# Gates of the first batch joined to the second's, ranks beside counts, independent stores, late records

## The chip, the cores and the metric

One core of a Trainium2 chip runs the whole program. The metric is the device time of one execution in microseconds (us). TensorE (PE) multiplies, VectorE (DVE), ScalarE (ACT) and GpSimd (POOL) do elementwise work, SyncE (SP) issues most of the DMAs. PSUM is the memory that TensorE writes, SBUF the one that all engines read.

## The reference

```python
scores = scale * np.matmul(q, k.transpose(0, 1, 3, 2)) - np.log(S)   # (8, 12, 448, 448), head_dim 64
attn = 1.0 / (1.0 + np.exp(-scores))
x = np.matmul(attn, v)            # then laid out as (3584, 768): 8 batches of 448 tokens
logits = x @ w_gate               # 8 experts
expert_idx = np.argmax(logits, axis=1)
gate_w = probs[np.arange(N), expert_idx]          # softmax of the logits
for e in range(E):                # w1 (8, 768, 1024), w2 (8, 1024, 768)
    mask = expert_idx == e
    out[mask] = gate_w[mask, None] * (np.maximum(x[mask] @ w1[e], 0.0) @ w2[e])
```

## The kernel before

**Attention.** Twelve heads make six pairs a batch. Two pairs advance together in steps of 64 keys, seven steps (ST) to two pairs, 21 (PB) to a batch, 168 in all; a step is called s below. `scores(s)` multiplies 64 by 64 quarters of k with 448 columns of q into two PSUM tiles named sc, `squash` makes the sigmoid on ScalarE, `weighted(s)` multiplies with v into av. `tokens` transposes av on VectorE into xt and writes it to x_tok in DRAM; `copy_tokens` keeps a copy in SBUF for the logits. `turn` transposes k and q on VectorE.

**Gates.** For each batch b: `gate_a` makes the logits (24 records on TensorE, line 291), `gate_b` transposes them (two matmuls, L300) and finds each token's expert (oh, one hot) on VectorE, `gate_c` counts the tokens of each expert with a matmul over ones (L335), finds the commonest expert and says which batch fills the next dense slot, `gate_c2` marks which tokens go elsewhere (lm), `gate_c3` makes the gate factors. `gate_d` numbers the tokens that go elsewhere: two matmuls into pr, one over the upper triangle for the rank within a group, one over ones for the totals (L388, L389), and a chain of additions on VectorE that reads pr (L392 to L403). `gate_d2` scatters four records per batch with GpSimd (L424). The small PSUM tiles of these steps share the four buffers of sc.

**Experts.** Seven dense slots (NS) each hold one batch's 448 tokens and the commonest expert of it. `moe` works in three passes of 128 by 128 matmuls over split weights (high and low part): L240 for the first layer, L263 for the second. ScalarE makes the high part of a weight, GpSimd the low one (L160). L247 and L248 free an expert PSUM tile (two buffers) and make the high and low part of the hidden values. What stays over is done at the end by lists of records.

**Order.** Everything is in an order written out by hand: `attention` yields, and `more(7)` puts seven expert matmuls in between. Before s = 70 (START) there are no expert matmuls; after it, seven steps of attention come in one burst (i == BURST), and expert matmuls fill the rest. PLACES says at which s a gate step stands: EARLY for the first two batches (first batch: b at 26, c and c2 at 28, c3 at 30, d at 32, its records at 34 to 40; second batch: b at 48, c at 50, the tokens' load l and c3 at 52, d at 54, records from 56 to 62), FIRST_LATE and LATE for the next five, LAST for the eighth. Each engine, and SyncE's queue, works in the order of the program. `store` issues an output store on SyncE; it waits for earlier stores unless `apart` has declared the two independent, which it does for stores of the same columns. `tokens` issues four writes of x_tok on SyncE as soon as a batch's half is transposed.

Of the kernel before, what the change touches and what calls it, by code (L numbers as in the profile page):

```python
# [9 lines left out]
F32 = mybir.dt.float32  # L10
F32R = mybir.dt.float32r
BF16 = mybir.dt.bfloat16
# [6 lines left out]
P = 128  # L19
NCH = 4  # L20
# [4 lines left out]
def tile_sigmoid_attention_top1_moe(  # L25
# [182 lines left out]
                self.split += 1  # L208

    stores = []  # L210
    stored = {}
# [12 lines left out]
    def moe(b, wts):  # L224

# [60 lines left out]
    def gate_a(b):  # L286
        psg = small_ps(b, "psg")
        for t in range(KD):
            for h in range(2):
                n = t % 2 * 2 + h  # L290
                nc.tensor.matmul(
                    psg[32 * n : 32 * (n + 1), :GH], wg[:, t], wholes[b, t][:, h * GH : (h + 1) * GH],
                    start=(t < 2), stop=(t >= KD - 2),
                )
        nc.vector.tensor_copy(logits, psg[:, :GH])

    def gate_b(b):
        pl = small_ps(b, "pl")
# [28 lines left out]
    def gate_c(b, oh, z):  # L327
        def tl(nm, shape, dt=F32):
            return small.tile(shape, dt, tag=nm, name=f"{nm}_{b}")

        s1, s2 = tl("s1", [GP, NCH, E]), tl("s2", [GP, NCH, E])
        nc.scalar.activation(s1, z, AF.Sigmoid)
        nc.scalar.activation(s2, z, AF.Sigmoid, scale=-1.0)
        pc = small_ps(b, "pc")
        nc.tensor.matmul(pc[:, : NCH * E], ones[:GP], oh.rearrange("p c e -> p (c e)"), start=True, stop=True)  # L335
        cnt = tl("cnt", [P, E])
        nc.vector.tensor_reduce(cnt, pc[:, : NCH * E].rearrange("p (c e) -> p e c", e=E), axis=AX.X, op=ALU.add)
        cm = tl("cm", [P, 1])
        nc.vector.tensor_reduce(cm, cnt, axis=AX.X, op=ALU.max)
        ce = tl("ce", [P, E])  # L340
        nc.vector.scalar_tensor_tensor(ce, cnt, cm, rev, op0=ALU.is_equal, op1=ALU.mult)
        cr, was, now = top[:, b : b + 1], free[:, b : b + 1], free[:, b + 1 : b + 2]
        nc.vector.tensor_reduce(cr, ce, axis=AX.X, op=ALU.max)
        ri = tl("ri", [P, 2], I32)
        if b > 0:
            rf = tl("rf", [P, 2])
            old = top[:, b - 1 : b]
            nc.vector.tensor_sub(rf[:, 0:1], old, cr)
            nc.vector.scalar_tensor_tensor(rf[:, 0:1], rf[:, 0:1], was, cr, op0=ALU.mult, op1=ALU.add)
            nc.vector.tensor_scalar(ri[:, 0:1], rf[:, 0:1], -1.0, float(E), op0=ALU.mult, op1=ALU.add)  # L350
            nc.vector.tensor_scalar(ri[:, 1:2], was, -1.0, float(b), op0=ALU.mult, op1=ALU.add)
        return s1, s2, ri, ce, cm

    def gate_c2(b, oh, s1, s2, ri, ce, cm):
# [12 lines left out]
        nc.vector.tensor_scalar(ce, ce, keep, 1.0, op0=ALU.mult, op1=ALU.add)  # L367
        lm = tl("lm", [GP, NCH, E], BF16)
        nc.vector.tensor_tensor(lm, oh, ce[:GP].unsqueeze(1).broadcast_to([GP, NCH, E]), op=ALU.mult)
        return lm  # L370

    def gate_c3(b, s1, s2):
        nc.vector.reciprocal(s2, s2)
# [6 lines left out]
    def gate_d(b, lm):  # L380
# [10 lines left out]
        tot = pr[:, nce : 2 * nce].rearrange("p (c e) -> p c e", e=E)  # L391
# [12 lines left out]
        return si  # L404
# [47 lines left out]
    xts = {}  # L452
    wholes = {}
    raws = {}
    taken = [[] for _ in range(4)]
    x_tok_b = x_tok.rearrange("(b j r) (i f) -> b i r j f", b=B, r=32, i=4)

    def load_slot(n, ri):

        regs[n] = nc.sync.value_load(ri[0:1, 0:1], min_val=0, max_val=E - 1)  # L460
        maps[n] = nc.sync.value_load(ri[0:1, 1:2], min_val=0, max_val=B - 1)
        raws[n] = xpool.tile([P, S // 32, KD, 32], F32, tag="raw", bufs=1, name=f"raw_{n}")
        for i in range(4):
            got = nc.sync.dma_start(
                raws[n][32 * i : 32 * (i + 1)].rearrange("r j t s -> r j (t s)"),
                x_tok_b[bass.ds(maps[n], 1), i].rearrange("o r j f -> (o r) j f"),
            )
            taken[i].append(got)

    low_parts = []  # L470

# [16 lines left out]
    def tokens(g, pv):  # L488
# [5 lines left out]
            xts[b] = xtpool.tile([P, NB, KH, 32], F32, tag="xt", bufs=2, name=f"xt_{b}_{n}")  # L494
        nc.vector.transpose(xts[b][:, :, t, :], pv[:, :S].rearrange("p (j s) -> p j s", s=32))  # L495
        if t == KH - 1:
            rows = x_tok[b * S : (b + 1) * S].rearrange("(j r) (i f) -> i r j f", r=32, i=4)
            for i in range(4):
                put = nc.sync.dma_start(
                    rows[i][:, :, n * KH * 32 : (n + 1) * KH * 32],  # L500
                    xts[b][32 * i : 32 * (i + 1)].rearrange("r j t s -> r j (t s)"),
                )
# [170 lines left out]
    def attention():  # L673
# [32 lines left out]

        def stage(what, b):
            g = gate.setdefault(b, {})
            if what == "b":
                g["oh"], g["z"] = gate_b(b)  # L710
            elif what == "c":
                g["c"] = gate_c(b, g["oh"], g["z"])
# [4 lines left out]
            elif what == "l" and b > 0:  # L717
                load_slot(b - 1, g["c"][2])
            elif what == "d":
                si_of[b] = gate_d(b, g["lm"])  # L720
# [6 lines left out]

        LATE = {8: "b", 10: "c", 11: ("l", "c2"), 12: "c3", 15: "d", 16: "g", 26: "e"}
        FOUR = ("s0", "s1", "s2", "s3")
        PUTS = 2 * (dict(zip((13, 15, 17, 19), FOUR)),) + 4 * (dict(zip((27, 28, 29, 30), FOUR)),)  # L730
        PUTS += (dict(zip((25, 26, 27, 28), FOUR)), {9: "s0", 10: "s1"})
        LAST = {3: "b", 5: "c", 6: ("l", "c2"), 7: "c3", 8: "d", 9: "g"}
        EARLY = {5: "b", 7: ("c", "c2"), 9: ("l", "c3"), 11: "d", 13: "g", 32: "e"}
        FIRST_LATE = {8: "b", 10: "c", 11: ("l", "c2"), 12: "c3", 15: "d", 16: "g", 26: "e"}
        PLACES = {}
        for b in range(B):
            places = (EARLY, EARLY, FIRST_LATE, LATE, LATE, LATE, LATE, LAST)[b]
            for r, what in [*places.items(), *PUTS[b].items()]:
                at = (b + 1) * PB + r
                at += at < START and at % 2  # L740
# [19 lines left out]
        for s in range(N_ST + 11):  # L760
# [33 lines left out]
            if s in SPLITS:  # L794
                split_tokens(0, SPLITS.index(s), nc.vector.tensor_copy)
            yield s, MIX[1]
        order.close()

    wts = Weights([(lambda b=b: regs.get(b)) for b in range(B + 1)], NS)
# [382 lines left out]
```

## Time and profile before

| what | value |
|---|---|
| time of three runs | median 776.97 us (776.0 to 777.6) |
| the profiled execution | 776.84 us, span 775.0 us |
| PE busy | 768.4 us (99%), 5586 matmuls |
| DVE, ACT, POOL busy | 373.9, 384.1, 349.6 us (48%, 50%, 45%) |
| PE clock granted | 1.000 |
| DMA | 125.67 MB, 162 GB/s |

The span runs from the first to the last instruction; the profiled execution's time has 1.84 us around it. A matmul's end in the trace is modelled, so the busy share says little about how densely the matmuls follow each other: the starts do. An fp32 matmul is recorded twice.

### The profile page before, as it was taken

The numbers are of one execution on the slowest core, as the hardware profiler recorded it, in microseconds if no ns is written. First come the engines' busy times: TensorE is split into PE (matmuls) and PEld (weight loads), VectorE is DVE, ScalarE is ACT, GpSimd is POOL, SyncE is SP. The second block draws the span as 40 slices with busy tenths as digits, with TensorE's granted clock in tenths as the row PEclk, the third lists the DMA queues.
The fourth block names the chain that finished last, engine by engine and source line by source line (L and its number), as shares of the span: only waits on it lengthen the run. The fifth ranks groups of instructions, "written<-read, shape, count | busy, mean of one in ns | idle before, by whom it ended". The sixth has DMA issues, their size and how long they took to land. (4 is left out here: it accounts for less than half of the span.)

```text
span 775.0 us, 15532 instructions
## 1 busy us (share of the span) xinstructions
PE 768.4 (99%) x5586; PEld 593.3 (77%) x5586; DVE 373.9 (48%) x806; ACT 384.1 (50%) x688; POOL 349.6 (45%) x330
## 2 busy tenths in 40 slices
PE   9999999999999999999999999999999999999997
PEld 6555557687696786867868769677698999999996
DVE  2354584465264652537426384254736493244543
ACT  5877776645536455264443653545523342444451
POOL 8648554242352342531615316054265764664351
PEclk9999999999999999999999999999999999999999
DMA  9777798976758846587585876766167554655770
GB/s 207 169 160 157 171 251 197 210 171 154 169 129 173 201 107 166 139 190 168 116 194 84 193 169 144 183 168 166 38 171 170 157 146 118 202 143 155 220 223 38
DMA packets 311633, 125.67 MB, mean 162 GB/s; under 512 B 210062, under 2 KB 307006, under 8 KB 311552
## 3 DMA queue, kind: packets, MB, share of 16 engines
q1 hardware_dynamic: 305504, 112.42, 61.9%
q0 software_dynamic: 5760, 11.76, 5.4%
q8 instruction: 45, 0.74, 0.4%
q10 hardware_dynamic: 288, 0.46, 0.2%
q14 instruction: 36, 0.29, 0.1%
HBM read 102.49 MB, written 22.49 MB: 161 GB/s over the span
## 5 line engine op out<-in xcount | busy, mean ns | idle before, releaser
L602 ACT ACTIVATE at<-sc,bias_s 128x448 f32<-128x448 f32 x336 | 192.3, 633 | 107.4 <-PE sc L616 106.5
L160 POOL TENSOR_TENSOR w1l<-wst,w1h 128x768 fp32r<-128x768 f32 x72 | 132.7, 1853 | 173.9 <-ACT w1h L159 172.2
L160 POOL TENSOR_TENSOR w2l<-wst,w2h 128x512 fp32r<-128x512 f32 x84 | 107.0, 1298 | 138.7 <-ACT w2h L159 121.0
L616 PE MATMUL sc<-qt,kt 64*64 64x448 f32 x1344 | 167.3, 545 | 0.0
L632 PE MATMUL av<-at,vn 64*64 64x448 f32 x1344 | 165.0, 536 | 0.0
L240 PE MATMUL ps<-xh,w1h 128*128 128x448 f32 x336 | 124.4, 370 | 0.2 <-DVE nw L439 0.2
L240 PE MATMUL ps<-xh,w1l 128*128 128x448 f32 x336 | 123.4, 367 | 0.0
L240 PE MATMUL ps<-xl,w1h 128*128 128x448 f32 x336 | 123.3, 367 | 0.0
L263 PE MATMUL ps<-hh,w2l 128*128 128x448 f32 x336 | 123.3, 367 | 0.0
L263 PE MATMUL ps<-hl,w2h 128*128 128x448 f32 x336 | 123.2, 367 | 0.0
L263 PE MATMUL ps<-hh,w2h 128*128 128x448 f32 x336 | 122.7, 365 | 0.0
L616 PEld LDWEIGHTS sc<-qt,kt 64*64 64x64 f32 x1344 | 78.2, 189 | 56.9 <-issue 44.4
L632 PEld LDWEIGHTS av<-at,vn 64*64 64x64 f32 x1344 | 59.4, 133 | 64.3 <-issue 53.5
L159 ACT CAST w2h<-wst 128x512 fp32r<-128x512 f32 x108 | 64.7, 620 | 75.7 <-PE ps L263 64.5
L247 ACT ACTIVATE hh<-ps 128x448 fp32r<-128x448 f32 x56 | 30.6, 546 | 139.6 <-PE ps L240 137.0
L276 DVE TENSOR_TENSOR ps<-ps,gt 128x448 f32<-128x448 f32 x42 | 40.7, 969 | 85.4 <-PE ps L263 85.3
L495 DVE STREAM_TRANSPOSE xt<-av 128x448 f32<-128x448 f32 x46 | 27.3, 629 | 101.5 <-PE av L632 100.4
L248 DVE SCALAR_TENSOR_TENSOR hl<-ps,hh 128x448 fp32r<-128x448 f32 x56 | 34.4, 614 | 78.3 <-ACT hh L247 76.8
L240 PEld LDWEIGHTS ps<-xh,w1h 128*128 128x128 f32 x336 | 63.1, 188 | 9.9 <-issue 4.4
L263 PEld LDWEIGHTS ps<-hh,w2l 128*128 128x128 f32 x336 | 65.2, 194 | 6.6 <-issue 3.5
L263 PEld LDWEIGHTS ps<-hl,w2h 128*128 128x128 f32 x336 | 65.2, 194 | 6.2 <-issue 3.2
L263 PEld LDWEIGHTS ps<-hh,w2h 128*128 128x128 f32 x336 | 65.2, 194 | 3.4 <-DVE nw L439 0.2
(158 smaller groups left out, 918.9 us busy)
## 6 DMA issues: line engine op xcount, KB each, us to landing
wst<-in_moe_w_dram SPq DMA_DIRECT2D x72, 384.0 KB, 3.3
wst<-in_moe_w_dram SPq DMA_DIRECT2D x54, 512.0 KB, 5.1
x_tok<-xt SPq DMA_DIRECT2D x64, 168.0 KB, 2.8
qn<-in_q_dram SPq DMA_DIRECT2D x184, 56.0 KB, 3.1
raw<-x_tok SPq DMA_DIRECT2D x28, 336.0 KB, 6.2
out_dram<-ob SPq DMA_DIRECT2D x84, 112.0 KB, 2.4
kn<-in_k_dram SPq DMA_DIRECT2D x104, 56.0 KB, 3.3
kn<-in_k_dram POOLq DMA_DIRECT2D x80, 56.0 KB, 4.0
```

The source lines that it names most:

```text
L159: nc.scalar.copy(hi, st)
L160: eng.tensor_tensor(lo, st, hi.bitcast(F32), op=ALU.subtract)
L240: nc.tensor.matmul(ps[:, :S], a[:, ws], b_, start=(t == 0 and n == 0), stop=(t == KD - 1 and n == 2))
L247: nc.scalar.activation(hh[:, :S], ps[:, :S], AF.Relu)
L248: nc.vector.scalar_tensor_tensor(hl[:, :S], ps[:, :S], 0.0, hh[:, :S].bitcast(F32), op0=ALU.max, op1=ALU.subtract)
L263: nc.tensor.matmul(ps[:, :S], a, b_, start=(j == 0 and n == 0), stop=(j == KF - 1 and n == 2))
L276: nc.vector.tensor_tensor(by_gate, by_gate, gate_rows[b], op=ALU.mult)
L495: nc.vector.transpose(xts[b][:, :, t, :], pv[:, :S].rearrange("p (j s) -> p j s", s=32))
L602: nc.scalar.activation(at, ps[:, :S], AF.Sigmoid, bias=bias_s, scale=SCALE)
L616: nc.tensor.matmul(ps[quarter(g, h), :S], ks, ops[g, "q"][OWN[h]], start=True, stop=True)
L632: nc.tensor.matmul(psv[g][OWN[h], :S], ops[g, "v"][rows, c, :], at[rows], start=(c == 0), stop=(c == KC - 1))
```

## The change

Of the first batch only the logits are made at its place (into logits_0). The second batch's places do all other gate steps for both: four transposes, operations over twice the columns, two counting matmuls, no rank matmuls. In batches 3 to 8 the rank matmul runs beside the counting one, over oh instead of lm, and the results are copied to SBUF (sums). The records of the first batch move from s = 34, 36, 38, 40 to 70, 72, 74, 76, those of the second from 56 to 62 to 80, 82, 84, 86. All output stores are declared independent of each other, all token writes of all token loads; the token writes are issued behind the next seven expert matmuls. An empty instruction on SyncE stands ahead of each store and each group of token writes. The working tiles of the joined steps lie in two buffers that the hidden values use later (h0).

```diff
     def store():
...
+            nc.sync.nop()
             put = nc.sync.dma_start(
...
-            apart(put, stored.setdefault((d, i), []))
+            apart(put, stored)
...
-        nc.vector.tensor_copy(logits, psg[:, :GH])
+        nc.vector.tensor_copy(logits_0 if b == 0 else logits, psg[:, :GH])
...
+    def early_b():
+        pl = small_ps(1, "pl")
+        for b, lo in enumerate((logits_0, logits)):
+            for c in range(2):
+                at = (2 * b + c) * P
+                nc.tensor.transpose(pl[:GP, at : at + P], lo[:, c * GP : (c + 1) * GP], ident)
...
+    def early_c(oh, z):
...
+        for n, of in enumerate((ones, upper)):
+            nc.tensor.matmul(
+                pc[:, n * n2 : (n + 1) * n2], of[:GP], oh.rearrange("p c e -> p (c e)"), start=True, stop=True
+            )
+        sums = early[1][:, GH : GH + 2 * n2]
+        nc.vector.tensor_copy(sums, pc[:, : 2 * n2])
...
-        nc.tensor.matmul(pc[:, : NCH * E], ones[:GP], oh.rearrange("p c e -> p (c e)"), start=True, stop=True)
+        nce = NCH * E
+        for n, of in enumerate((ones, upper)):
+            nc.tensor.matmul(
+                pc[:, n * nce : (n + 1) * nce], of[:GP], oh.rearrange("p c e -> p (c e)"), start=True, stop=True
+            )
+        sums = tl("sums", [P, 2, NCH, E])
+        nc.vector.tensor_copy(sums.rearrange("p n c e -> p (n c e)"), pc[:, : 2 * nce])
...
+        nc.vector.tensor_mul(cnt, cnt, ce)
...
-        pr = small_ps(b, "pr")
-        lmf = lm.rearrange("p c e -> p (c e)")
-        nce = NCH * E
-        nc.tensor.matmul(pr[:, :nce], upper[:GP], lmf, start=True, stop=True)
-        nc.tensor.matmul(pr[:, nce : 2 * nce], ones[:GP], lmf, start=True, stop=True)
...
-            nc.vector.tensor_add(pre[:, c], pre[:, c - 1], tot[:, c - 1])
-        nc.vector.tensor_add(base, pre[:, NCH - 1], tot[:, NCH - 1])
+            nc.vector.tensor_add(pre[:, c], pre[:, c - 1], sums[:, 0, c - 1])
+        nc.vector.tensor_add(base, base, cnt)
...
-        nc.vector.tensor_add(rk, pre[:GP], pr[:GP, :nce].rearrange("p (c e) -> p c e", e=E))
+        nc.vector.tensor_add(rk, pre[:GP], sums[:GP, 1])
...
+            to_keep.append((b, n, xts[b]))
...
+    def keep_tokens():
+        while to_keep:
+            b, n, xt = to_keep.pop(0)
...
-                for got in taken[i]:
+                for got in taken:
                     tc.declare_no_dep(put.ins, got.ins, reason="the slots read earlier batches' tokens")
...
-        PUTS = 2 * (dict(zip((13, 15, 17, 19), FOUR)),) + 4 * (dict(zip((27, 28, 29, 30), FOUR)),)
+        PUTS = tuple(dict(zip(range(r, r + 8, 2), FOUR)) for r in (START - PB, START + 10 - 2 * PB)) + 4 * (dict(zip((27, 28, 29, 30), FOUR)),)
...
-        EARLY = {5: "b", 7: ("c", "c2"), 9: ("l", "c3"), 11: "d", 13: "g", 32: "e"}
+        EARLY = {5: "B", 7: "C", 9: ("l", "C3"), 11: "D", 13: "g", 32: "e"}
...
-            places = (EARLY, EARLY, FIRST_LATE, LATE, LATE, LATE, LATE, LAST)[b]
+            places = ({}, EARLY, FIRST_LATE, LATE, LATE, LATE, LATE, LAST)[b]
...
             yield s, MIX[0]
+            keep_tokens()
```

## Rows read from the trace of the kernel before

**Rows 1.** Waits of TensorE, whole span: total us, times, longest.

```profile
PE ps_warm L593 <- DVE ones L76: 1.1, 1, 1.1
PE ps L240 <- DVE nw L439: 0.2, 1, 0.2
```

**Rows 2.** Timeline of TensorE, first batch's gates: start us, us, instructions, count.

```profile
45.09 1.34 PE L291 MATMUL psg<-xf,wg 128*32 128x224 f32 x24
46.36 1.79 PE L616 MATMUL sc<-qt,kt 64*64 64x448 f32 x16
...
49.61 0.43 PE L300 MATMUL pl<-ident,logits 128*112 128x128 f32 x2
49.97 1.79 PE L616 MATMUL sc<-qt,kt 64*64 64x448 f32 x16
...
63.21 2.02 PE L616 MATMUL sc<-qt,kt 64*64 64x448 f32 x16
...
76.74 1.27 PE L632 MATMUL av<-at,vn 64*64 64x448 f32 x8
...
81.74 1.34 PE L291 MATMUL psg<-xf,wg 128*32 128x224 f32 x24
```

**Rows 3.** The same, first row of the stretch that ends at 45.09 (rows 2).

```profile
11.55 1.66 PE L616 MATMUL sc<-qt,kt 64*64 64x448 f32 x12
```

**Rows 4.** The same, first row and end of the second batch's stretch.

```profile
83.01 1.79 PE L616 MATMUL sc<-qt,kt 64*64 64x448 f32 x16
...
115.71 1.34 PE L291 MATMUL psg<-xf,wg 128*32 128x224 f32 x24
```

**Rows 5.** The same, third batch's counting and rank matmuls among expert matmuls.

```profile
135.85 0.37 PE L240 MATMUL ps<-xh,w1h 128*128 128x448 f32 x1
136.06 0.19 PE L335 MATMUL pc<-oh,ones 112*128 112x32 bf16 x1
...
136.38 0.37 PE L240 MATMUL ps<-xh,w1l 128*128 128x448 f32 x1
...
161.37 0.37 PE L240 MATMUL ps<-xl,w1h 128*128 128x448 f32 x1
161.58 0.19 PE L388 MATMUL pr<-lm,upper 112*128 112x32 bf16 x1
...
161.93 0.36 PE L240 MATMUL ps<-xh,w1h 128*128 128x448 f32 x1
```

**Rows 6.** The same, first and last rows of stretches of 55 expert matmuls.

```profile
149.90 0.47 PE L240 MATMUL ps<-xh,w1h 128*128 128x448 f32 x1
...
244.41 0.47 PE L240 MATMUL ps<-xh,w1h 128*128 128x448 f32 x1
...
255.66 0.37 PE L240 MATMUL ps<-xl,w1h 128*128 128x448 f32 x1
```

**Rows 7.** Timelines of VectorE (alone, beside a split) and GpSimd (the split).

```profile
87.40 0.19 DVE L317 TENSOR_TENSOR eq<-lg,mx 112x32 f32<-112x32 f32 x1
...
131.52 1.45 DVE L317 TENSOR_TENSOR eq<-lg,mx 112x32 f32<-112x32 f32 x1
...
131.09 1.84 POOL L160 TENSOR_TENSOR w1l<-wst,w1h 128x768 fp32r<-128x768 f32 x1 [5.13 <-ACT w1h L159]
```

**Rows 8.** Timelines: a late operation of a rank chain; an expert tile's release and use.

```profile
352.19 1.20 DVE L399 TENSOR_TENSOR rk<-rk,lm 112x32 f32<-112x32 f32 x1
...
259.34 0.58 DVE L248 SCALAR_TENSOR_TENSOR hl<-ps,hh 128x448 fp32r<-128x448 f32 x1
...
259.97 0.48 PE L263 MATMUL ps<-hh,w2h 128*128 128x448 f32 x1
```

**Rows 9.** Waits of SyncE's queue, the longest: total us, times, longest.

```profile
SPq L218 <- DMA out_dram<-ob: 82.2, 50, 5.9
```

**Rows 10.** Timelines of VectorE and TensorE ahead of the first expert matmuls.

```profile
102.47 1.18 DVE L495 STREAM_TRANSPOSE xt<-av 128x448 f32<-128x448 f32 x2 [2.02 <-PE av L632]
...
117.46 0.62 DVE L570 STREAM_TRANSPOSE qt<-qn 128x448 f32<-128x448 f32 x1
...
120.10 1.70 PE L616 MATMUL sc<-qt,kt 64*64 64x448 f32 x16
```

**Rows 11.** Busy time of VectorE in that stretch: us, DVE busy (operations), clock, DMA.

```profile
102.47:118.08 15.61, 15.20 (x29) 1.00 1.14 258
```

More of the change, by code (lines that the diff above doesn't have):

```diff
@@ L294, in gate_a, with both @@
                 )
-        nc.vector.tensor_copy(logits, psg[:, :GH])
+        nc.vector.tensor_copy(logits_0 if b == 0 else logits, psg[:, :GH])
+    early = [hpool.tile([P, 2 * S], F32, tag=f"h{x}0", name=f"early_{x}") for x in "hl"]
+    logits_0 = early[1][:, :GH]
+    cuts = {}
+    def both(nm, n, words=None):
+        if nm not in cuts:
+            at = cuts.get("at", 0)
+            cuts[nm], cuts["at"] = early[0][:, at : at + (words or n)], at + (words or n)
+            assert cuts["at"] <= 2 * S
+        return cuts[nm]
@@ new lines, in both_e, with per_c, bc @@
+    def both_e(nm, n=1):
+        return both(nm, 2 * NCH * E).rearrange("p (c e) -> p c e", e=E)
+    def per_c(ce):
+        return ce[:GP].rearrange("p (b e) -> p b e", e=E).unsqueeze(2).broadcast_to([GP, 2, NCH, E])
+    def early_b():
[4 more added lines that the diff above has]
+                nc.tensor.transpose(pl[:GP, at : at + P], lo[:, c * GP : (c + 1) * GP], ident)
+        plv = pl[:GP].rearrange("p (c t h e) -> p c t h e", c=4, t=2, h=2)
+        sh = [GP, 2 * NCH, E]
+        def bc(a):
+            return a.unsqueeze(2).broadcast_to(sh)
+        lg, eq, z = (both_e(nm)[:GP] for nm in ("lg", "eq", "z"))
+        mx, mr = (both(nm, 2 * NCH)[:GP] for nm in ("mx", "mr"))
+        oh = both("oh", 2 * NCH * E, NCH * E).bitcast(BF16).rearrange("p (c e) -> p c e", e=E)[:GP]
+        lgv = lg.rearrange("p (c h) e -> p c h e", c=4)
+        nc.vector.tensor_copy(lgv, plv[:, :, 0, :, :E])
+        nc.vector.tensor_add(lgv, lgv, plv[:, :, 1, :, :E])
+        nc.vector.tensor_reduce(mx, lg, axis=AX.X, op=ALU.max)
+        nc.vector.tensor_tensor(eq, lg, bc(mx), op=ALU.is_equal)
+        nc.vector.tensor_tensor(eq, eq, rev[:GP].unsqueeze(1).broadcast_to(sh), op=ALU.mult)
+        nc.vector.tensor_reduce(mr, eq, axis=AX.X, op=ALU.max)
+        nc.vector.tensor_tensor(oh, eq, bc(mr), op=ALU.is_equal)
+        nc.vector.tensor_tensor(z, lg, bc(mx), op=ALU.subtract)
+        return oh, z
@@ new lines, in early_c @@
+    def early_c(oh, z):
+        s1, s2 = (both_e(nm)[:GP] for nm in ("s1", "s2"))
+        nc.scalar.activation(s1, z, AF.Sigmoid)
+        nc.scalar.activation(s2, z, AF.Sigmoid, scale=-1.0)
+        pc = small_ps(1, "pc")
+        n2 = 2 * NCH * E
+        for n, of in enumerate((ones, upper)):
[4 more added lines that the diff above has]
+        nc.vector.tensor_copy(sums, pc[:, : 2 * n2])
+        sums = sums.rearrange("p (n b c e) -> p n b c e", n=2, b=2, e=E)
+        cnt, cm, ce, keep = both("cnt", 2 * E), both("cm", 2), both("ce", 2 * E), both("keep", 2)
+        cnt_b, ce_b = (x.rearrange("p (b e) -> p b e", e=E) for x in (cnt, ce))
+        sh = [P, 2, E]
+        nc.vector.tensor_reduce(cnt_b, sums[:, 0].rearrange("p b c e -> p b e c"), axis=AX.X, op=ALU.add)
+        nc.vector.tensor_reduce(cm, cnt_b, axis=AX.X, op=ALU.max)
+        nc.vector.tensor_tensor(ce_b, cnt_b, cm.unsqueeze(2).broadcast_to(sh), op=ALU.is_equal)
+        nc.vector.tensor_tensor(ce_b, ce_b, rev.unsqueeze(1).broadcast_to(sh), op=ALU.mult)
+        nc.vector.tensor_reduce(top[:, :2], ce_b, axis=AX.X, op=ALU.max)
+        for b in range(2):
+            was, now, kept = free[:, b : b + 1], free[:, b + 1 : b + 2], keep[:, b : b + 1]
+            nc.vector.scalar_tensor_tensor(kept, cm[:, b : b + 1], float(2 * P), was, op0=ALU.is_le, op1=ALU.mult)
+            nc.vector.tensor_sub(now, was, kept)
+        rf = both("rf", 1)
+        ri = small.tile([P, 2], I32, tag="ri", name="ri_1")
+        was = free[:, 1:2]
+        nc.vector.tensor_sub(rf, top[:, 0:1], top[:, 1:2])
+        nc.vector.scalar_tensor_tensor(rf, rf, was, top[:, 1:2], op0=ALU.mult, op1=ALU.add)
+        nc.vector.tensor_scalar(ri[:, 0:1], rf, -1.0, float(E), op0=ALU.mult, op1=ALU.add)
+        nc.vector.tensor_scalar(ri[:, 1:2], was, -1.0, 1.0, op0=ALU.mult, op1=ALU.add)
+        return ri, oh, ce, keep, cnt, sums
@@ new lines, in early_c2 @@
+    def early_c2(oh, ce, keep, cnt):
+        ce_b = ce.rearrange("p (b e) -> p b e", e=E)
+        nc.vector.tensor_tensor(ce_b, ce_b, top[:, :2].unsqueeze(2).broadcast_to([P, 2, E]), op=ALU.is_equal)
+        nc.vector.tensor_scalar(keep, keep, -1.0, None, op0=ALU.add)
+        for b in range(2):
+            nc.vector.tensor_scalar(ce_b[:, b], ce_b[:, b], keep[:, b : b + 1], 1.0, op0=ALU.mult, op1=ALU.add)
+        lm = both("lm", 2 * NCH * E).rearrange("p (b c e) -> p b c e", b=2, e=E)[:GP]
+        nc.vector.tensor_tensor(lm, oh.rearrange("p (b c) e -> p b c e", b=2), per_c(ce), op=ALU.mult)
+        nc.vector.tensor_mul(cnt, cnt, ce)
+        return lm
@@ L297, in gate_b, with early_c3 @@
+    def early_c3():
+        s1, s2 = (both_e(nm)[:GP] for nm in ("s1", "s2"))
+        nc.vector.reciprocal(s2, s2)
+        nc.vector.tensor_mul(s1, s1, s2)
+        sm = both("sm", 2 * NCH)[:GP]
+        nc.vector.tensor_reduce(sm, s1, axis=AX.X, op=ALU.add)
+        nc.vector.tensor_scalar(sm, sm, 1e-9, None, op0=ALU.add)
+        nc.vector.reciprocal(gates[:GP, :2].rearrange("p b c -> p (b c)"), sm)
     def gate_b(b):
@@ L367, in gate_c2 @@
         nc.vector.tensor_scalar(ce, ce, keep, 1.0, op0=ALU.mult, op1=ALU.add)
-        lm = tl("lm", [GP, NCH, E], BF16)
+        lm = tl("lm", [GP, NCH, E])
         nc.vector.tensor_tensor(lm, oh, ce[:GP].unsqueeze(1).broadcast_to([GP, NCH, E]), op=ALU.mult)
-        return lm
+        nc.vector.tensor_mul(cnt, cnt, ce)
+        return lm, sums, cnt
     def gate_c3(b, s1, s2):
@@ L454, in tile_sigmoid_attention_top1_moe @@
     raws = {}
-    taken = [[] for _ in range(4)]
+    taken = []
     x_tok_b = x_tok.rearrange("(b j r) (i f) -> b i r j f", b=B, r=32, i=4)
@@ L708, in stage @@
             g = gate.setdefault(b, {})
-            if what == "b":
+            if what == "B":
+                g["oh"], g["z"] = early_b()
+            elif what == "C":
+                ri, *g["early"] = early_c(g["oh"], g["z"])
+                g["c"] = None, None, ri
+            elif what == "C3":
+                oh, ce, keep, cnt, sums = g["early"]
+                g["lm"] = early_c2(oh, ce, keep, cnt)
+                early_c3()
+            elif what == "D":
+                oh, ce, keep, cnt, sums = g["early"]
+                for n in range(2):
+                    si_of[n] = gate_d(n, g["lm"][:, n], sums[:, :, n], cnt[:, n * E : (n + 1) * E])
+            elif what == "b":
                 g["oh"], g["z"] = gate_b(b)
@@ L796, in attention @@
             yield s, MIX[1]
+        keep_tokens()
         order.close()
```

19 lines of the change are left out of this document (10 added, 9 removed).

## The prediction

> **What bounds the kernel now.** I read the waits of TensorE first. In the whole span it waits 1.3 us for another engine, 1.1 of it once at the start [rows 1]. So VectorE, ScalarE, GpSimd and the DMA queues end no stretch of it. The end moves only with the time TensorE itself needs, or if one of the others becomes late.
>
> The second view is TensorE's timeline, read for its pitch, because a busy share of 99% does not show a matmul that takes longer than it must. In the attention stage an undisturbed stretch, from 63.21 to 76.74, starts 144 score and value matmul records in 13.53 us: 0.094 us each [rows 2]. Against that pitch I measure every stretch between two logit matmuls. From 46.36 to 81.74 (first batch: its three small gate steps lie in it) 352 records start in 35.38 us; at the pitch they need 33.06, so 2.32 us are lost [rows 2]. From 11.55 to 45.09, where no gate matmul lies, 350 records take 33.54 and need 32.88: 0.66 lost [rows 3]. From 83.01 to 115.71 (second batch) 320 records take 32.70 and need 30.06: 2.64 lost [rows 4]. So small gate matmuls among the 64 by 64 ones cost far more than their own length; the two transposes of the first batch stand for 0.36 of the 2.32 (49.61 to 49.97).
>
> In the mixed stage the neighbours are full 128 by 128 matmuls, and the loss is small. Around the counting matmul, 135.85 to 136.38 holds two expert matmuls and takes 0.53, where two at 0.205 take 0.41: 0.12. Around the two rank matmuls, 161.37 to 161.93 takes 0.56: 0.15 [rows 5]. A second small matmul in the same place thus costs about 0.03.
>
> **The change, part by part.**
>
> *First batch's gates joined to the second's.* At its place only the logits (24 records, and VectorE's copy) stay. Transposes, counting and rank matmuls go: three breaks in the stretch from 46.36. What is left is a stretch like that of rows 3: 2.32 less 0.66 is 1.66. That one does not begin right behind a matmul of another shape, so I take 1.55. Bounds: only the matmuls' own time goes, 0.36 + 0.12 + 0.15 = 0.63; or the whole 2.32.
>
> *Second batch.* Three breaks lose 2.64 less 0.66, 1.98, or 0.66 each. The rank break goes: 0.6 won. The break of the transposes grows by two more. The two of the first batch took 0.36 with the entry into the break, which is paid once; bounds for two more are 0.06 (twice 0.03, rows 5) and 0.36; I take 0.25, nearer to their own row. The counting matmul becomes two, over 64 columns: 0.04. Net gain 0.3, bounds 0.1 and 0.5. By the Trainium skill (TensorE: Matmul & The Clock Gate, section Back-to-back issue gap) matmuls of 128 columns would follow each other at about 56 ns at full clock. By that the two transposes are an estimated 0.11 and the sum would be 0.14 better. No row here shows transposes that close, and the row decides.
>
> *Ranks beside counts, third to eighth batch.* The matmul with the upper triangle moves beside the counting one, the second one over the ones goes. Per batch 0.12 + 0.15 becomes about 0.15 (two in one place, rows 5): 0.11, six times, 0.65. Bounds 0.3 and 1.0.
>
> *VectorE's work.* Each joined operation covers twice the columns; one on 32 columns takes 0.19 [rows 7], one on 64 between that and twice that. The second batch's chain grows by some 16 operations (6 before the slot is known, a second run of the rank chain of 10), some 3.5 us, and the first batch's chain goes. Its cover is VectorE's idle time there, 2.02 us ahead of 102.47 alone [rows 10]. Without it, what is queued behind is the turning of k and q, the last of which is read by the scores at 120.10 and ends at 118.08: 2.0 us of room [rows 10]. I cost it at nothing. In the third to eighth batch a copy and a product are added, and the additions of the rank chain now read their second operand from SBUF (sums) instead of PSUM (pr). That is the costly point. A VectorE operation with both operands in SBUF takes 0.19 alone, but 1.45 where a GpSimd split runs beside it: it ends with that split (131.09 and 1.84) [rows 7]. This is what the Trainium skill says of an instruction with two SBUF inputs beside a GpSimd one that reads SBUF (SBUF — State Buffer, section Who interferes with whom); the trace agrees, 1.45 against 0.19. Five more operations a batch are open to it. Behind them on VectorE waits the subtraction that frees an expert PSUM tile. In one batch it ends at 259.92 and TensorE starts the matmul that needs the tile at 259.97 [rows 8]: no room. At another place TensorE already waits 0.2 us on that chain [rows 1]. Against it, the chain no longer waits for the rank matmuls. Bounds: 0.2 won (TensorE's wait of today), or at each of three places a wait for one whole split, 1.84, 5.5 lost. I charge 0.25, near the lower end: operations further down the same chain, with both operands in SBUF, wait for these splits already today (1.20 instead of 0.19, at 352.19 [rows 8]), so most of the waiting is not added but only comes earlier in the chain.
>
> *Records late.* Eight record scatters leave GpSimd's queue between the k and v loads and go among the weight splits behind 120 us. They and their iota issue there without touching TensorE; the queue they enter is idle part of the time. Two index tiles rotate, so the third batch's rank chain now waits for the first batch's last scatter, which stands two steps ahead of it: 28 expert matmuls at 0.205, 5.7 us. The joined steps' tiles are wanted by the hidden values only behind the first expert matmuls, past 120.10, while the chain is over before 102.47 [rows 10]. Cost nothing; if that fails it delays the same chain, and lands within the bounds just given.
>
> *Stores independent, tokens kept later, the added nops.* SyncE waits 82.2 us in total, 50 times, for earlier output stores [rows 9]. These waits go, and weight loads behind them issue earlier. Since TensorE waits for no weight [rows 1], this is worth nothing; for the same reason half a step's delay of the token writes and some 100 empty instructions on SyncE cost nothing. What is late next is the splitting engines, as now.
>
> **Sum.** 1.55 + 0.30 + 0.65 - 0.25 = 2.25 us. The profiled execution took 776.84 us (span 775.0, 1.84 around it), so 774.6. It lies 0.1 below the median of the runs shown, 776.97; that does not change the figure.
>
> **The rivals.**
>
> *A: the slower pitch stays.* After a gate break the expert matmuls run at one of two pitches. 55 of them from 149.90 to 161.37 take 11.47, from 244.41 to 255.66 11.25: 0.22, or 4 ns each [rows 5, 6]. The first stretch follows a counting matmul and ends with the rank matmuls; after them the pitch is the faster one again. With the rank matmuls gone, a slow pitch could last through the other 55 or so up to the next burst. In five batches 109 matmuls (13 ahead of a burst, 55 and 41 behind it) at 4 ns are 2.2; some 0.8 of it, an estimate from the stretches that run slow today, is in the time now: 1.4 lost, 776.0. Against it: rank matmuls can also start the slow pitch, and a pair may set it otherwise than a single one.
>
> *B: VectorE is late at the start of the experts.* If the longer chain takes more than its idle time and slot 0's tokens come later, the 2.0 us of room goes, and the scores of 120.10 wait 1 to 2 us: 775.6 to 776.6, say 776.2. For it: from 102.47 to 118.08 VectorE is busy nearly all the time [rows 11]. Against it: the chain starts with an idle engine.
>
> *C: slower, the rank chain behind GpSimd's splits.* The price is worked out above: 776.84 - 2.5 + 5.5 = 779.8. It decides from the point where the subtraction behind the chain ends after TensorE's need by more than 1.4 in each of three places, which eats the 2.5 and 1.5 more. For it: no room at 259.97. Against it: where the subtraction belongs to the last tile of its layer there is room for a whole tile.
>
> *D: the change does not do what it says.* The lost time of the attention stage is not in the breaks but in how score and value matmuls overlap, and it is paid at the next logit matmul in any case. Then the first batch gives 0.63, the second nothing, the rest stays: 0.63 + 0.65 - 0.25 = 1.0, 775.8. Against it: the stretch of rows 3 ends in a logit matmul too and lost only 0.66.
>
> **How the numbers follow.** Forecast 0.60, A 0.13, B 0.09, C 0.10, D 0.08. What a measurement of this kernel can tell from no change is 0.2%, 1.55 us: so faster is below 775.4 and slower above 778.5. The forecast's own range is 773.4 to 775.4: the low end from the upper bounds of the first and third part (0.8 and 0.35 more). Of B and D a little lies below 775.4, which makes faster 0.64. Slower has C's 0.10; 0.26 remains. The range for 8 in 10 reaches to A, B and D and leaves out C: 773.2 to 776.9.
>
> **What would show it.** Right: on TensorE's timeline one unbroken stretch between the first two logit matmuls that loses under 0.9 us; four transposes and two counting matmuls in the second batch, no rank matmuls anywhere; two small matmuls in one place of each mixed batch, with an expert matmul lost there; TensorE's waits still near 1.3 us; SyncE's waits on output stores gone without effect. Wrong: a wait of TensorE for VectorE in the rank chain's places (C) or near 118 us (B); expert pitch of 0.207 through both layers of most batches (A); a loss near 1.7 us in the first stretch although nothing breaks it (D).

## The result, and the profile after

The changed kernel takes 781.83 us (median of 7 runs, 779.7 to 784.39), the kernel before 776.97 (7 runs, 776.0 to 777.6): ratio 1.0061, 95% interval 1.0045 to 1.0078. It is slower, by 0.6%; 774.6 was forecast. The profiled execution took 782.07 us, its span 780.3 against 775.0.

The first view is again TensorE's waits (total us, times, longest), kernel after:

```profile
PE ps L264 <- DVE nw L539: 1.7, 1, 1.7
PE sc L725 <- DVE logits L296: 1.7, 1, 1.7
PE ps_warm L702 <- DVE ones L76: 1.1, 1, 1.1
PE ps L241 <- DVE nw L539: 0.6, 1, 0.6
PE psg L292 <- ACT xf L763: 0.4, 1, 0.4
```

Of these the 1.1 at the start stood in the old list, and so did a wait of 0.2 on `nw` [rows 1]. The waits of 1.7, 1.7 and 0.4 are new, and the 0.2 has grown to 0.6: VectorE, which behind the start ended 0.2 us of waiting before, ends 4.0 now.

Second, TensorE's timeline from the first logits to the first expert matmuls (start us, us, instructions, count), kernel after:

```profile
45.12 1.34 PE L292 MATMUL psg<-xf,wg 128*32 128x224 f32 x24
...
80.07 1.34 PE L292 MATMUL psg<-xf,wg 128*32 128x224 f32 x24
...
84.59 0.43 PE L321 MATMUL pl<-ident,early_l 128*112 128x128 f32 x2
84.85 0.38 PE L321 MATMUL pl<-ident,logits 128*112 128x128 f32 x2
85.17 1.79 PE L725 MATMUL sc<-qt,kt 64*64 64x448 f32 x16
...
113.46 0.96 PE L292 MATMUL psg<-xf,wg 128*32 128x224 f32 x16
114.79 1.10 PE L292 MATMUL psg<-xf,wg 128*32 128x224 f32 x8 [0.37 <-ACT xf L763]
115.83 1.78 PE L725 MATMUL sc<-qt,kt 64*64 64x448 f32 x12
119.26 0.65 PE L725 MATMUL sc<-qt,kt 64*64 64x448 f32 x2 [1.65 <-DVE logits L296]
...
126.98 0.47 PE L241 MATMUL ps<-xh,w1h 128*128 128x448 f32 x1
```

From the first logits to the second it now takes 34.95 us where it took 36.65 [rows 2], and to the third 33.39 where it took 33.97 [rows 4]. That is 2.28 won. Then the stretch from the third logits to the first expert matmul takes 13.52; before it was 10.08 (115.71 to 125.79).

Laying the same landmarks over the whole span (starts on TensorE's timelines of the two profiled executions; each row goes from the landmark above it to its own) shows where the 5.3 us are:

| stretch | before | after | difference |
|---|---|---|---|
| to the first logits | 45.09 | 45.12 | +0.03 |
| first to third batch's logits | 70.62 | 68.34 | -2.28 |
| to the first expert matmul | 10.08 | 13.52 | +3.44 |
| to the first L264 matmul (L263 before) of slot 0 | 41.00 | 42.92 | +1.92 |
| to the fourth batch's logits | 34.45 | 36.11 | +1.66 |
| fourth to eighth batch's logits | 367.97 | 368.03 | +0.06 |
| to the last three matmuls of the dense slots | 130.51 | 130.69 | +0.18 |
| rest of the span | 75.28 | 75.57 | +0.29 |

**First place, 113 to 127 us.** VectorE, GpSimd and ScalarE there (timelines, kernel after):

```profile
115.16 0.60 DVE L577 STREAM_TRANSPOSE whole<-raw 128x448 f32<-128x448 f32 x1
...
116.22 2.15 DVE L581 TENSOR_TENSOR xl<-whole,xh 128x448 fp32r<-128x448 f32 x1
...
118.86 0.35 DVE L296 COPY logits<-psg 128x224 f32<-128x224 f32 x1
...
116.09 1.81 POOL L160 TENSOR_TENSOR w1l<-wst,w1h 128x768 fp32r<-128x768 f32 x1 [5.18 <-ACT w1h L159]
...
114.21 1.06 ACT L763 COPY xf<-av 128x448 f32<-128x448 f32 x2 [1.19 <-DVE xt L595]
```

The subtraction and the copy of the logits, kernel before (timeline of VectorE):

```profile
116.08 0.63 DVE L481 TENSOR_TENSOR xl<-whole,xh 128x448 fp32r<-128x448 f32 x1
...
117.19 0.35 DVE L295 COPY logits<-psg 128x224 f32<-128x224 f32 x1
```

The last of slot 0's token splits (transpose, cast, subtraction: the steps listed in `SPLITS`) stands on VectorE ahead of the copy of the logits, and the scores of 119.26 need the PSUM buffer that this copy empties. The logit matmuls come 2.25 us earlier than before, the splits do not: before, they began at 104.10, directly behind a transpose; now they begin at 104.26, where VectorE has waited 0.59 us for slot 0's tokens to land. The subtraction, which took 0.63, takes 2.15 beside a GpSimd split. So the copy, at 117.19 before, is at 118.86. The logit matmuls themselves are held too: from their first to the scores behind them it takes 2.37 us (113.46 to 115.83) instead of 1.27 [rows 4]. They wait for ScalarE's copy xf, and that waits for VectorE's transpose xt, which stands among the same splits. So 1.10 of the 3.44 are lost ahead of 115.83, where no subtraction is held up yet, and 2.34 behind it; the 1.52 by which the subtraction is longer can only be in the second part.

**Second place, 162 to 174 us.** The third batch's rank chain, then GpSimd, then TensorE (timelines, kernel after):

```profile
162.07 3.50 DVE L494 TENSOR_TENSOR pre<-pre,sums 128x8 f32<-128x8 f32 x3
...
165.83 1.17 DVE L498 TENSOR_TENSOR rk<-rk,region 112x32 f32<-112x32 f32 x1
167.04 1.20 DVE L499 TENSOR_TENSOR rk<-rk,lm 112x32 f32<-112x32 f32 x1
...
169.26 0.58 DVE L249 SCALAR_TENSOR_TENSOR hl<-ps,hh 128x448 fp32r<-128x448 f32 x1
...
161.63 0.95 POOL L524 DMA_INDIRECT recs<-rec,si  x1 [0.15 <-issue]
162.60 2.54 POOL L160 TENSOR_TENSOR w2l<-wst,w2h 128x512 fp32r<-128x512 f32 x2
165.61 2.59 POOL L160 TENSOR_TENSOR w2l<-wst,w2h 128x512 fp32r<-128x512 f32 x2 [0.47 <-DMA x_tok<-xt]
...
169.90 0.48 PE L264 MATMUL ps<-hh,w2h 128*128 128x448 f32 x1 [1.74 <-DVE nw L539]
```

The additions in the kernel before:

```profile
161.83 0.56 DVE L394 TENSOR_TENSOR pre<-pre,pr 128x8 f32<-128x8 f32 x3 [1.05 <-PE pr L389]
```

Three additions that took 0.56 take 3.50 and end with the pair of splits; two operations below are caught by the next pair. The subtraction `hl` queued behind the chain is late, and TensorE stands for 1.74 us. One thing is special to this batch: a late scatter of the first batch's records (161.63) stands on GpSimd directly ahead of the pair. In the fifth batch no scatter does (timelines, kernel after):

```profile
356.08 2.59 DVE L494 TENSOR_TENSOR pre<-pre,sums 128x8 f32<-128x8 f32 x3
...
355.89 2.56 POOL L160 TENSOR_TENSOR w2l<-wst,w2h 128x512 fp32r<-128x512 f32 x2 [1.19 <-ACT w2h L159]
```

There two additions are held for one split each, none for both, the next operations find GpSimd idle, and TensorE waits for nothing; so it is in the sixth and seventh batch, and in the fourth one addition is held. What follows the stop is seen in the windows (us, then per engine busy us and operations: PE, PEld, DVE, ACT, POOL; granted clock, DMA share, GB/s), kernel after:

```profile
169.90:172.00 2.10, 2.10 (x7) 1.88 (x8) 2.03 (x6) 0.00 (x0) 0.00 (x0) 0.61 0.66 110
172.00:174.00 2.00, 2.00 (x7) 1.80 (x6) 1.90 (x5) 0.00 (x0) 0.96 (x1) 0.55 0.66 158
174.00:176.00 2.00, 2.00 (x17) 1.28 (x20) 1.27 (x3) 0.00 (x0) 0.00 (x0) 1.00 1.10 371
```

Directly behind the stop the granted clock is near 0.5, the lower of its two levels (1.2 GHz), and the matmuls start 0.37 us apart instead of 0.20. That is the 1.66 of the next stretch. **Third**, in the last batch TensorE waits 0.6 (600.79) instead of 0.2 (595.80).

**Where 0.65 was to be won.** From the fourth to the eighth batch's logits the time is the same, though no rank matmuls break in. The third and the last matmul of a first-layer stretch behind an attention burst (timeline of TensorE, kernel after):

```profile
249.73 0.37 PE L241 MATMUL ps<-xh,w1l 128*128 128x448 f32 x1
...
264.61 0.37 PE L241 MATMUL ps<-xh,w1l 128*128 128x448 f32 x1
```

That is 72 steps of 206.7 ns, the slower of the two pitches that the prediction names under rival A. In the kernel after, all five of these stretches (third to seventh batch; 81, 75, 69, 63 and 57 matmuls) keep it to the end of the layer. In the kernel before, only those of the third and sixth batch start at it, the others at 202.7, and in the third to sixth batch, where enough matmuls follow the rank matmuls to tell, the pitch changes there to the other one. In the run "ranks as before" below it is again the third and the sixth batch that start at the slower pitch.

### The profile page after: what moved, and what is told of

The parts are those of the page before. It is cut to its first block, busy times and chain, and to the rows that moved or that the text cites. A ratio compares the mean times of both kernels' runs of the same rounds, so it can differ in the third digit from the quotient of the medians.

```text
span 780.3 us, 15500 instructions
## 1 busy us (share of the span) xinstructions
PE 769.2 (99%) x5576; PEld 598.5 (77%) x5576; DVE 387.7 (50%) x801; ACT 384.3 (49%) x686; POOL 348.4 (45%) x330
## 5 line engine op out<-in xcount | busy, mean ns | idle before, releaser
L725 PE MATMUL sc<-qt,kt 64*64 64x448 f32 x1344 | 170.7, 543 | 1.7 <-DVE logits L296 1.7
L741 PE MATMUL av<-at,vn 64*64 64x448 f32 x1344 | 167.7, 536 | 0.0
L725 PEld LDWEIGHTS sc<-qt,kt 64*64 64x64 f32 x1344 | 80.6, 189 | 59.5 <-issue 45.9
L264 PE MATMUL ps<-hh,w2h 128*128 128x448 f32 x336 | 123.5, 368 | 1.7 <-DVE nw L539 1.7
L264 PE MATMUL ps<-hh,w2l 128*128 128x448 f32 x336 | 123.9, 369 | 0.0
L264 PE MATMUL ps<-hl,w2h 128*128 128x448 f32 x336 | 123.8, 369 | 0.0
L264 PEld LDWEIGHTS ps<-hh,w2l 128*128 128x128 f32 x336 | 65.6, 195 | 6.7 <-issue 3.5
L264 PEld LDWEIGHTS ps<-hl,w2h 128*128 128x128 f32 x336 | 65.6, 195 | 6.3 <-issue 3.2
L264 PEld LDWEIGHTS ps<-hh,w2h 128*128 128x128 f32 x336 | 65.6, 195 | 5.7 <-DVE nw L539 2.4
```

Source lines behind the costliest of these rows:

```text
L264: nc.tensor.matmul(ps[:, :S], a, b_, start=(j == 0 and n == 0), stop=(j == KF - 1 and n == 2))
L725: nc.tensor.matmul(ps[quarter(g, h), :S], ks, ops[g, "q"][OWN[h]], start=True, stop=True)
L741: nc.tensor.matmul(psv[g][OWN[h], :S], ops[g, "v"][rows, c, :], at[rows], start=(c == 0), stop=(c == KC - 1))
```

## Experiments

My theory: two losses independent of each other, VectorE's queue ahead of the copy at 119 us and the rank chain beside GpSimd's splits at 162. The rivals: the longer chain of the two joined batches (B); the late record scatter ahead of those splits; the changes on SyncE. No run of the changed kernel puts the records alone back to their old places. Each ratio is to runs of the kernel before on the same chip.

**The rank chain earlier.** The changed kernel, third to seventh batch: the chain stands right behind the marks (lm) instead of four steps later.

```diff
-        LATE = {8: "b", 10: "c", 11: ("l", "c2"), 12: "c3", 15: "d", 16: "g", 26: "e"}
+        LATE = {8: "b", 10: "c", 11: ("l", "c2", "d"), 12: "c3", 16: "g", 26: "e"}
```

`FIRST_LATE` is edited likewise, and `si` has three buffers.

> The changed kernel, with the rank chain of the third to seventh batch (line 492 to 503) moved from its own place to directly behind the marks (c2), ahead of the attention burst, where VectorE has 8.3 us and GpSimd 11.7 us idle; the index tile gets a third buffer. Theory 1 (two places lose the time: near 118 us VectorE is late, near 168 us the rank chain stands behind GpSimd's weight splits and the halved clock after that stop costs as much again): TensorE's wait of 1.7 us at 168 and the half clock up to 174 go, 781.8 - 1.8 - 1.7 = 778.3; the loss near 118 stays. Theory 2 (the SyncE parts cost: independent stores and late token writes crowd the DMA engines, landings of token writes went from 2.8 to 5.8 us): 781.8 as it is.

778.33 us; ratio 1.0025 (1.0015 to 1.0035). Its waits, of TensorE:

```profile
PE sc L725 <- DVE logits L296: 1.7, 1, 1.7
...
PE ps L241 <- DVE nw L539: 0.6, 1, 0.6
PE psg L292 <- ACT xf L763: 0.4, 1, 0.4
```

Only the stop at 168 us is gone, and the half clock with it. In the new place, where no split runs beside them, the additions are short although they read SBUF:

```profile
143.07 0.57 DVE L494 TENSOR_TENSOR pre<-pre,sums 128x8 f32<-128x8 f32 x3
```

**Token splits later.** The changed kernel; the last two steps of VectorE's token splits go behind the logits. (They are VectorE's splits of slot 0's tokens, three operations each. Where an expectation calls them weight splits, as those of the last two runs do, that is wrong: GpSimd's weight splits are issued by other steps.)

```diff
-    SPLITS = (START - 12, START - 11, START - 10, START - 9, START - 8, START - 6)
+    SPLITS = (START - 12, START - 11, START - 10, START - 9, START - 2, START - 1)
```

> The changed kernel, with the last two of the six token splits of slot 0 moved from steps 62 and 64 to 68 and 69, behind the turning of k and q and the copy of the logits on VectorE, which then has 5.1 us idle. Theory 1: the stretch from the third batch's logit matmuls to the first expert matmul goes from 13.5 us back to about 10.1, TensorE's waits of 1.65 and 0.4 near 118 go: 781.8 - 3.4 = 778.4; the stop near 168 stays. Theory 2: 781.8.

778.89 us; ratio 1.0024 (1.0014 to 1.0034). From the third logits (113.63) to the first expert matmul (123.71) it takes 10.08 us, as before the change, and the wait on the logits is gone. The stop of 1.74 in the third batch is still there, with a small new one:

```profile
PE ps L264 <- DVE nw L539: 1.7, 1, 1.7
...
PE ps L241 <- DVE hl L249: 0.7, 1, 0.7
PE ps L241 <- DVE nw L539: 0.6, 1, 0.6
```

**Ranks as before.** The changed kernel, but `gate_c`, `gate_c2` and `gate_d` of the third to eighth batch are those of the kernel before: two rank matmuls into `pr`, the additions read PSUM.

```diff
+        nc.tensor.matmul(pr[:, :nce], upper[:GP], lmf, start=True, stop=True)
+        nc.tensor.matmul(pr[:, nce : 2 * nce], ones[:GP], lmf, start=True, stop=True)
...
+            nc.vector.tensor_add(pre[:, c], pre[:, c - 1], tot[:, c - 1])
...
+        nc.vector.tensor_add(rk, pre[:GP], pr[:GP, :nce].rearrange("p (c e) -> p c e", e=E))
...
-                si_of[b] = gate_d(b, *g["lm"])
+                si_of[b] = gate_d_pr(b, g["lm"])
```

> The changed kernel, with the gates of the third to eighth batch as before the change: two rank matmuls into pr, the chain's additions read PSUM. Records, stores, token writes and the joined first two batches stay changed. Theory 1: the chain no longer stands behind the splits from its first addition on, the stop at 168 (1.7) and the half clock (1.7) go, two small matmuls a batch come back (0.1 each): 778.3 to 779. A rival for the stop (the first batch's last record scatter pushes GpSimd's splits into the chain): the scatter is still there, so the stop stays, 781.8.

777.8 us; ratio 1.0015 (1.0006 to 1.0025), a little better than expected. The stop in the third batch is gone, the one on the logits stays. VectorE and GpSimd in the third batch:

```profile
161.78 0.56 DVE L513 TENSOR_TENSOR pre<-pre,pr 128x8 f32<-128x8 f32 x3 [1.05 <-PE pr L508]
...
162.67 1.23 DVE L517 TENSOR_TENSOR rk<-rk,region 112x32 f32<-112x32 f32 x1
...
160.33 0.95 POOL L543 DMA_INDIRECT recs<-rec,si  x1 [0.15 <-issue]
161.29 2.55 POOL L160 TENSOR_TENSOR w2l<-wst,w2h 128x512 fp32r<-128x512 f32 x2
```

The scatter is in its late place and the pair of splits right behind it, and the three additions inside that pair take 0.56: one operand comes from PSUM. The next operation with both in SBUF takes 1.23. So the scatter by itself does not hold additions that read PSUM. The form of the operands decides whether an addition is held, as the tile views of `pre` (count: shortest/median/longest ns) say for the whole span, kernel before first, then kernel after:

```profile
L394 DVE TENSOR_TENSOR pre<-pre,pr x24: 161/161/165, 60.2 to 592.6; 128x8 f32<-128x8 f32 x24
```

```profile
L494 DVE TENSOR_TENSOR pre<-pre,sums x18: 166/168/3099, 162.1 to 597.3; 128x8 f32<-128x8 f32 x18
```

None of 24 additions from PSUM was stretched, nor any of the 18 in the run with the ranks as before (longest 164 ns). Of 18 from SBUF eight were: one took 3.10 us, seven took 1.15 to 1.21. By lines the first sum to 3.9 us, mean 162 ns, the second to 13.0 us, mean 725 ns. The seven stopped TensorE nowhere. So whether the SBUF operands would have stopped it in the third batch without the scatter ahead of the pair isn't shown.

**SBUF operands alone.** The kernel before; VectorE copies the ranks to SBUF and the chain reads the copy.

```diff
-        tot = pr[:, nce : 2 * nce].rearrange("p (c e) -> p c e", e=E)
+        prs = tl("prs", [P, 2 * nce])
+        nc.vector.tensor_copy(prs, pr[:, : 2 * nce])
+        tot = prs[:, nce : 2 * nce].rearrange("p (c e) -> p c e", e=E)
```

The addition of `pr` to `pre` reads `prs` too.

> The kernel before, where only the rank matmuls' result (pr) is first copied to SBUF and the rank chain reads the copy: one copy more a batch, the same matmuls at the same place. Theory 1 (additions with both operands in SBUF stand behind GpSimd's splits): single additions of 1 to 3 us in the third batch's chain, TensorE waits 1 to 3 us in all instead of 1.3 at the start alone, 778 to 780. Rival (it is the place or the scatters, not the operand): 0.2 us a batch on VectorE only, 776.6.

779.09 us; ratio 1.0033 (1.002 to 1.0046).

```profile
PE ps L263 <- DVE nw L441: 1.1, 1, 1.1
...
PE ps L240 <- DVE nw L441: 0.9, 1, 0.9
```

The 1.1 is in the fourth batch, at the matmul that had no room [rows 8] (261.45 now); the 0.9 in the last. The size came out, but not by the operations expected: of the 24 additions to `pre`, all from SBUF here, one was stretched (1.21 at 353.62, fifth batch), none in the third batch. The operations that are caught at these two places are ones further down that read SBUF before as well (1.29 at 257.82, 1.87 at 594.86): against the split they come some 0.3 us later than before (257.23 and 257.55 before, 257.82 and 257.78 now; 593.08 and 593.35, 594.86 and 594.84) and no longer slip in ahead of it. So this run shows how little room there is; the effect of the operands is shown by the run before it and the two tile views.

**SyncE alone.** The kernel before with the changed stores, tokens kept later and empty instructions only:

```diff
-            apart(put, stored.setdefault((d, i), []))
+            apart(put, stored)
...
-            taken[i].append(got)
+            taken.append(got)
...
+            keep_tokens()
```

> The kernel before, with only SyncE's parts of the change: empty instructions, stores independent, token writes independent of all loads and issued later. Theory 1: SyncE's waits on output stores go, TensorE does not notice: 777.0, within 0.2%. Theory 2: the loss of the change or a good part of it, 779 to 782.

776.39 us; ratio 0.9999 (0.999 to 1.0009). SyncE's 82.2 us of waits on output stores [rows 9] are gone and TensorE's waits are those of before.

**The joined chain elsewhere.** The changed kernel, the rank chains of the first two batches moved from the stretch ahead of the tokens' landing to two steps ahead of the experts (`11: "D"` to `26: "D"` in `EARLY`). If rival B's longer chain makes VectorE late, the wait on the logits must go.

> The changed kernel, with the two joined rank chains of the first two batches (3.5 us on VectorE near 97) moved from step 54 to step 68, behind the turns. It tells why VectorE is late at 118: if the longer gate chain ahead of 102 does it (the prediction's rival B), 3 us come back, 778.5; if VectorE's dense stretch only begins when slot 0's tokens land at 104.3 and is as long as before, while TensorE comes 2.25 us earlier, the wait near 118 stays, 781.8.

781.47 us; ratio 1.0061 (1.0047 to 1.0076). The wait of 1.7 stays: VectorE waited 2.49 us for the tokens (104.88) and was late all the same. The length of the rank chains is not the cause. The run leaves the other half of rival B, that slot 0's tokens come later: from the second batch's counting matmuls to the end of the slot's choice on VectorE it takes 3.79 us (88.41 to 92.20) where it took 2.69 (89.87 to 92.56), and the load of the tokens stands behind that. By the row at 104.26 this can have cost the splits 0.59 at most.

**Both cures**, chain earlier and token splits later.

> The changed kernel with both mends: the rank chain of the third to seventh batch directly behind the marks (third index tile), and the last two token splits of slot 0 behind the turns. Theory 1: both losses go and are independent, 781.8 - 3.5 - 2.9 = 775.4 by the two measured singly; TensorE waits 1.7 us in all, 0.6 of it in the last batch; 0.15% under the kernel before. If the two overlap (one only makes room for the other), 777 to 778.

777.65 us; ratio 1.0007 (0.9997 to 1.0016). The profiled execution took 775.49 with waits of 1.1, 0.6 and 0.4; the other executions lie between 775.45 and 779.02, and what the longer ones add isn't seen in the one profiled. So it isn't shown that the two losses simply add up. **With the last batch's chain moved too** (`LAST` as `LATE`):

> The one before, and in the last batch too the rank chain directly behind the marks. Theory 1: TensorE's wait of 0.6 in the last batch goes, 0.6 less than the kernel with both mends, 774.8. Against it: there is no attention burst there, and the subtraction that frees an expert tile stands right behind the marks; if the chain of 1.8 us holds it up past TensorE's need, a new wait of up to 1.8 takes the place of the 0.6.

776.78 us; ratio 1.0006 (0.9995 to 1.0018). The last wait only changed its name (`hl`, 0.6 at 590.38, for `nw`, 0.6 at 593.93).

**Joined first gates, ranks from PSUM, token splits later.** The two sound parts together: the run "ranks as before" with the later token splits; beside it the same with only the last of the two splits moved.

> The joined gates of the first two batches stay, the third to eighth batch have the rank matmuls of the kernel before (their chain reads PSUM again), and the last two weight splits ahead of the experts stand six and five steps later. If the two stops named so far (the logits copy at 119 us, the chain beside the splits at 168 us) are all that the change costs: no wait of TensorE over 1 us behind the start, first expert matmul near 123.4, and the profiled execution 1.5 to 2 us under the kernel before, 774.8 to 775.5, the median with it. If the later splits themselves bring the spread of the executions that the kernel with both cures showed (775.5 to 779), the profiled execution is about 775 and the median 776 to 777.5.

> As the kernel beside it, but only the last of the two splits moves, the other stays where the change has it. If the wait at 119 us came from the split that runs beside the subtraction of VectorE at 116 us, and that is the one left in place, the subtraction still takes about 2 us and TensorE waits 1 to 1.7 us: 776.5 to 777.5. If it is the one moved, the wait goes and the time is that of the kernel beside it, 774.8 to 775.5. If only the landing of the tokens decides (VectorE dense from 104 us), the wait is 0.3 to 0.7 in both.

The first: 775.55 us, ratio 0.9982 (0.9972 to 0.9991), faster than both kernels, by little. Its TensorE waits:

```profile
...
PE turn_k L709 <- DMA kn<-in_k_dram: 0.2, 1, 0.2
PE ps L241 <- DVE nw L558: 0.2, 1, 0.2
```

Its copy of the logits waits for TensorE, no longer the other way round:

```profile
114.04 0.39 DVE L296 COPY logits<-psg 128x224 f32<-128x224 f32 x1 [1.13 <-PE psg L292]
```

The profiled execution took 774.28, 2.56 less than that of before; 0.76 of it lies ahead of the first logits (44.33 against 45.09), where TensorE's order was not changed; that place varies from 44.08 to 45.57 over the profiled executions. The second: 776.1, ratio 0.999 (0.9981 to 0.9999). The wait on the logits is gone there too, so the last token split was what the copy waited behind. Its stretch from the logits (112.38) to the expert matmuls (123.31) is still 0.85 longer than 10.08, all of it in the logit matmuls, and a stop of 1.1 in the third batch is left. This stop is the late records' (timelines of VectorE and TensorE):

```profile
163.50 0.85 DVE L522 TENSOR_SCALAR si<-sl 112x4 uint32<-112x4 f32 x1 [1.70 <-DMA recs<-rec,si]
...
165.47 0.47 PE L264 MATMUL ps<-hh,w2h 128*128 128x448 f32 x1 [1.12 <-DVE nw L558]
```

The rank chain, though its additions read PSUM, waits 1.70 us for a scatter of the first batch's records to free the index tile. GpSimd issues that scatter at 157.79, and the chain wants the tile at 161.80.

## Why the prediction was wrong, step by step

- **First and second batch's gates: right.** 1.85 was summed (1.55 and 0.30); 1.70 and 0.58 were measured, and the first stretch without gate steps loses about what rows 3 said. Rival D falls.
- **"VectorE's work ... I cost it at nothing": this step failed, 3.44 us.** It set the 2.0 us of room [rows 10] against the longer chain only. The room was used up by the gain itself: TensorE came 2.25 us earlier to a VectorE whose splits begin no earlier than before. Beside that, the subtraction moved under a GpSimd split (1.52 us more). Rival B had the place, and half of its mechanism is ruled out: the run with the rank chains moved keeps the wait; the tokens' landing can stand for 0.59 at most. The run with later token splits gives the 3.44 back. At least 1.10 of it is not the collision; how the other 2.34 divide between the collision and the earlier TensorE isn't separated.
- **"I charge 0.25": the term mis-sized.** At the third batch alone the chain beside the splits cost a stop of 1.74, about 1.7 in half clock behind it, and 0.4 more came in the last batch. This is rival C's mechanism, with the price that its bound of 5.5 allowed, though in other places. At the matmul of 259.97, where the prediction saw no room, nothing was lost: the chain no longer waits 1.05 for the rank matmuls, and that pays there for additions 1.04 longer. The argument that such waits "only come earlier in the chain" was wrong: in the third batch the first addition waits for one pair of splits and two operations below for the next.
- **Late records, "Cost nothing": not borne out.** The step counted on 5.7 us between the first batch's last scatter and the third batch's chain. In the run with only the last token split moved, the chain wanted the index tile 4.0 us after the scatter began, waited 1.70 for it, and TensorE stood for 1.12. In the run "ranks as before" the same wait is 0.74 (up to 165.09) and TensorE waits for nothing there. In the changed kernel the chain is too late to wait for it; there a scatter stands ahead of the pair of splits that holds the chain, and its share of the stop of 1.74 is open.
- **Ranks beside counts: 0.65 was summed, nothing came.** From the fourth to the eighth batch's logits 368.03 us, before 367.97, and 367.94 in the fastest kernel, which has the rank matmuls of before. The rank break is gone and two small matmuls in one place do cost little more than one. What took the gain back is rival A: without rank matmuls the slower pitch lasts to the end of the layer. Between these logits 320 first-layer matmuls run at it, before 180; at 4 ns each that is an estimated 0.56 us, against the 0.44 that four batches at 0.11 were to win. What sets the pitch stays open.
- **SyncE: right at nothing**, by the SyncE run on the kernel before.
- **The sum.** -2.28 + 3.44 + 1.92 + 1.66 + 0.06 + 0.18 + 0.32 = 5.30, the 0.32 being the first and the last row of the table. It is that of the profiled execution. Slower had 0.10 of the chances, because the two VectorE places were each argued away with the timings of before.

## What to carry to other kernels

Where a change lets the bounding engine arrive earlier, room measured in the old trace shrinks by the gain: for each engine that it waits on next, ask whether that one's work comes earlier too or is tied to a landing. Here an operand moved from PSUM to SBUF exposed a VectorE addition of 0.17 us to GpSimd's splits, and the price was the rest of GpSimd's operations (1.15 to 3.10 us), not the addition's own length. Of a change in several parts, run each alone: here joining the gates won 2.28 us, lost 3.44 behind them until the token splits were moved, and the ranks, worth nothing by themselves, cost 3.6 in the third batch together with the late records.

## What was not expected of the hardware

- A VectorE addition of 0.17 us took 3.10 beside GpSimd, where one split takes 1.3: it started at 162.07, while the scatter was being issued (161.63 to 162.58), and lasted to the end of both splits behind it (165.14). The Trainium skill (SBUF — State Buffer, section Who interferes with whom) has the rule that two SBUF inputs contend with a GpSimd instruction that reads SBUF and that one, outside the two-port modes, does not; the runs agree (3.10 against 0.16). It also says that issue order decides who blocks. Here the addition is recorded 0.53 ahead of the splits and still comes last; whether the scatter ahead of them is the reason isn't shown.
- The half clock behind a stop isn't settled by the stop's length. After 1.74 us without work at 168 the granted clock was 0.61 and 0.55; in the run with later token splits, after an equal 1.74 in the same place, and in the run with the joined chain elsewhere, after 1.91, it stayed at 1.00. So some 1.7 us of the loss belong to some executions only. Of the seven runs of the changed kernel the three with a mean granted clock of 0.996 take 782.07 to 784.39, the four with 0.998 or 0.999 take 779.7 to 781.83.
